# Smaller key-value blocks that share TensorE: 60-feature groups in two column halves, and four 64x64 tiles at once

## The chip, the core and the metric

The kernel runs on one core of a Trainium2 chip. A core has five engines that run side by side: TensorE (PE in the profile; its weight loads are PEld), VectorE (DVE), ScalarE (ACT), GpSimd (POOL) and SyncE (SP), which here only issues DMAs. TensorE writes its results to PSUM, eight banks of 512 f32 columns on 128 partitions. The metric is the device time of one execution in microseconds. Before the change three runs took 263.54 to 263.64 us, the median being 263.59 us.

## What is computed

One input `x` of 2048 tokens by 640 features goes through two branches, which a gate per token mixes.

```python
g = sigmoid((x * gate_w).sum(-1, keepdims=True))
# branch A: linear attention, 32 heads of 20 features
q, k, v = x @ wqkv            # split into 32 heads
pq, pk  = phi(q), phi(k)      # phi(t) = t+1 where t > 0, else exp(t); plus 1e-6
kv = einsum("hsd,hse->hde", pk, v)      # one 20x20 matrix a head
z  = pk.sum over tokens
a  = (einsum(pq, kv) / (einsum(pq, z) + 1e-6)) @ wo
# branch B: MLP
h  = gelu(layernorm(x) @ w1);  hs = shifted(h) @ w2;  x1 = x + hs
b  = x1 + gelu(layernorm(x1) @ w3) @ w4
out = g * a + (1 - g) * b
```

The kernel never forms `v`. It sums G = x^T pk over all tokens (640x640), then takes the blocks of wv^T G that belong to one head each (`kv`), and multiplies them by the rows of `wo` of that head. The result M (640x640) turns the normalised queries straight into branch A's output: a = (pq / den) @ M.

## The kernel before

All instructions are recorded one after the other by a planner (`_Items.run`): work stands in named streams, each item with the items it depends on and a lag in us, and the planner takes the item that its own cost estimates let TensorE begin first. Each engine then carries out its list strictly in the recorded order; waits on semaphores are put in where the data or a PSUM bank demands it. SP's list is one such queue: a DMA that waits holds up every DMA recorded behind it. `bank()` and `pair()` hand out one or two PSUM banks.

The stages, in the order of TensorE's list: q and k projections with phi (up to about 54 us); the sums of G (`gt_step`, line 795); W1, with the kv products between its groups (`kvt_group`, line 950); W2 with the layernorm sums; W3 for four chunks of 512 tokens (`w3_group`); between W3's groups the products M (`m_group`); then per token tile branch A's product (`a_tile`) and W4 (`w4_tile`, line 1122), with the outputs going out by DMA. `mm_group` (line 613) issues nearly all matmuls, so that most rows of the profile carry that line.

Around the change:

- **kv.** The 640 features are cut into five groups of 120 (six heads) and one of 40 (two heads). For each group, five matmuls over the 128-row slices of `wv` and G leave a 128 by 120 block in PSUM. `lt_evac` copies it with a mask that keeps the heads' 20x20 blocks (`Lt`). The work is in two halves with a bank pair each.
- **M.** `m_group` multiplies each of the six blocks of `Lt` by its rows of `wo` (`wo_aug`, filled by `load_wvo`), 512 and 128 columns; ACT copies the result to `M_sb`, rows 0 to 119 of block j. The sixth block, 40 rows, goes to `Mt`; `m_tail` then puts 8 of its rows under each of the five blocks (rows 120 to 127) by five DMAs on SP's queue.
- **Queries.** `qn_sum` and `qn_scale` divide each query tile by its denominator on DVE and store it in the same order of features: five blocks of 120 plus 8. `qt_tile` transposes a tile by a DMA on SP's queue (`pqnT<-pq_tok`).
- **SP's queue in this stretch** also carries the transposes of the second layernorm's output, `t_xn` (`xnT<-xn`), 16 tiles, which W3 reads. POOL computes each tile (`normalize`) into one of three buffers.

`a_tile` reads all 128 rows of every block of `M_sb`, so the first of them waits for the DMAs of `m_tail`.

Of the kernel before, what the change touches and what calls it, by code (L numbers as in the profile page):

```python
# [11 lines left out]
D = 640  # L12
# [417 lines left out]
def _build(nc, A_x, A_wqkv, A_wo, B_w1, B_w2, B_w3, B_w4, gate_w, out, dbg=None, stop=None):  # L430
# [240 lines left out]
    def memset(engf, ap, val):  # L671
        return engf(lambda e: e.memset(ap, val), [], [ap])
# [53 lines left out]
    def load_wvo():  # L726
        dp = [k_done[11]]
        sch.dma("pool", wv[:, :, :], A_wqkv[:, 2 * D:3 * D].rearrange("(k p) f -> p k f", p=128), "wv", deps=dp)
        for r in range(6):
            n = min(R6, D - R6 * r)  # L730
            sch.dma("pool", wo_aug[0:n, r, :], A_wo[R6 * r:R6 * r + n, :], "wo", group_total=6, deps=dp)
# [5 lines left out]
    aselect(mask_t[0:120], ones_c[0:120, 0:120].rearrange("p (b d) -> p b d", b=6), [[-20, 6], [0, 20]], ALU.is_ge, 0, 1)  # L737
    aselect(mask[0:120], mask_t[0:120], [[20, 6], [0, 20]], ALU.is_ge, 19, -1)
    memset(pool, Lt[:], 0.0)
    memset(pool, wvf[:, KD * D:], 0.0)  # L740
    memset(pool, wo_aug[:, 5, :], 0.0)
    memset(pool, hsT[:, :, 0:4], 0.0)
    memset(pool, hsT[:, :, S:S + 4], 0.0)


    tags = {}
# [187 lines left out]
    kv_bank = {}  # L934

    def kvt_group(h):
        b = pair()
        kv_bank[h] = b
        bank_hold.update((b, b + 1))
        mms = []  # L940
        for q_, r in enumerate(range(4) if h == 0 else range(4, 6)):
            n = min(R6, D - R6 * r)
            for k in range(KD):
                mms.append((ps[:, b, R6 * q_:R6 * q_ + n], wvf[:, D * k + R6 * r:D * k + R6 * r + 128], GT[:, k, R6 * r:R6 * r + n],
                            q_ == 0 and k == 0, k == KD - 1))

        def fn(e):
            ins = None
            for o, l, r_, st_, sp_ in mms:
                ins = e.matmul(o, l, r_, start=st_, stop=sp_, skip_group_check=True)  # L950
            return ins
        pe(fn, [wvf[:, :], GT[:, :, :]], [ps[:, b, 0:480], ps[:, b + 1, 0:1]], cost=len(mms) * 60.0)

    def lt_evac(h):
        b = kv_bank[h]
        for q_, r in enumerate(range(4) if h == 0 else range(4, 6)):
            n = min(R6, D - R6 * r)
            src = ps[0:n, b, R6 * q_:R6 * q_ + n].rearrange("p (h m i) -> p h m i", m=5, i=4)
            msk = mask[0:n, 0:n // DH, :].rearrange("p h (m i) -> p h m i", i=4)
            if r < 5:  # L960
                dst = Lt[0:n, r, 0:n].rearrange("p (h m i) -> p h m i", m=5, i=4)
            else:
                dst = Lt[0:n, r, 0:n].rearrange("p (m h i) -> p h m i", m=5, i=4)
            tt(dve, dst, src, msk, ALU.mult)
        bank_hold.difference_update((b, b + 1))

    def m_group(r):
        n = min(R6, D - R6 * r)
        kr = R6 if r < 5 else 128
        b = pair()  # L970
        mm_group(ps[:, b, 0:512], [(Lt[0:kr, r, :], wo_aug[0:kr, r, 0:512])])
        mm_group(ps[:, b + 1, 0:128], [(Lt[0:kr, r, :], wo_aug[0:kr, r, 512:D])])
        src = psf[0:n, 512 * b:512 * b + D]
        dst = M_sb[0:n, r, :] if r < 5 else Mt[0:n, :]
        activation(dst, src, ACTF.Copy)

    def m_tail():
# [73 lines left out]
    def qn_scale(t):  # L1051
        sd = qn_slot[t]
        ts(dve, dnr[:, 0, sd, :], dnr[:, 0, sd, :], EPS_PHI, None, ALU.add, ALU.bypass)
        dve(lambda e: e.reciprocal(dnr[:, 1, sd, :], dnr[:, 0, sd, :]), [dnr[:, 0, sd, :]], [dnr[:, 1, sd, :]], cost=350.0)
        blk = pq_tok[:, t, :].rearrange("p (j c) -> p j c", c=128)
        main = (blk[:, :, 0:R6].rearrange("p j (a d) -> p j a d", d=DH),
                pq_tok[:, t + 1, 0:5 * R6].rearrange("p (j a d) -> p j a d", a=6, d=DH),
                dnr[:, 1, sd, 0:30].rearrange("p (j a) -> p j a", a=6).unsqueeze(3).to_broadcast([128, 5, 6, DH]), 850.0)
        tail = (blk[:, :, R6:128].rearrange("p m (h i) -> p h m i", i=4),
                pq_tok[:, t + 1, 5 * R6:D].rearrange("p (h m i) -> p h m i", h=2, i=4),  # L1060
                dnr[:, 1, sd, 30:32].unsqueeze(2).unsqueeze(3).to_broadcast([128, 2, 5, 4]), 150.0)
        for o, i0, i1, cost in (main, tail):
            dve(lambda e, o=o, i0=i0, i1=i1: e.tensor_tensor(o, i0, i1, ALU.mult),
                [i0, dnr[:, 1, sd, :]], [o], cost=cost)
# [215 lines left out]
```

## Time and profile before

| | |
|---|---|
| Median of three runs | 263.59 us |
| Profiled execution, whole time | 263.69 us |
| Its span, first to last instruction | 261.6 us |
| PE busy | 256.0 us, 98% of the span |
| DVE, ACT, POOL busy | 149.0, 106.8, 95.3 us |
| First matmul of the first `a_tile` | 140.55 us |

The profile page is of one execution; what is outside its span is 2.1 us. The timeline lists the instructions of an engine in order of time, neighbours of a kind merged: start, length, engine, line, operation, tiles, count, and in brackets how long the engine was idle before them and what ended that. `SPq` are the DMA issues on SP's queue: their length is the time that SP is taken by the issue, not the transfer. The chain is the work that ended last, followed back to the start.

### The profile page before, as it was taken

The numbers are of one execution on the slowest core, as the hardware profiler recorded it, in microseconds if no ns is written. First come the engines' busy times: TensorE is split into PE (matmuls) and PEld (weight loads), VectorE is DVE, ScalarE is ACT, GpSimd is POOL, SyncE is SP. The second block draws the span as 40 slices with busy tenths as digits, with TensorE's granted clock in tenths as the row PEclk, the third lists the DMA queues.
The fourth block names the chain that finished last, engine by engine and source line by source line (L and its number), as shares of the span: only waits on it lengthen the run. The fifth ranks groups of instructions, "written<-read, shape, count | busy, mean of one in ns | idle before, by whom it ended". The sixth has DMA issues, their size and how long they took to land.

```text
span 261.6 us, 4268 instructions
## 1 busy us (share of the span) xinstructions
PE 256.0 (98%) x1668; PEld 135.7 (52%) x1699; DVE 149.0 (57%) x267; ACT 106.8 (41%) x215; POOL 95.3 (36%) x150
## 2 busy tenths in 40 slices
PE   8999999999999999999999999999999999999996
PEld 4555555555555555554444545554455544455553
DVE  2497787899903699979995407992023410143332
ACT  1386767752355756684875140005500045100000
POOL 5003996849774018687753201230011100011000
PEclk9999999999999999999999999999999999999999
DMA  6885979660566895544766600232000020000211
GB/s 198 253 91 137 165 172 172 179 122 16 87 125 103 224 387 155 76 81 74 111 124 125 103 0 0 41 84 77 0 3 0 3 100 0 3 0 0 103 50 50
DMA packets 50612, 24.82 MB, mean 95 GB/s; under 512 B 41973, under 2 KB 49182, under 8 KB 50593
## 3 DMA queue, kind: packets, MB, share of 16 engines
q1 hardware_dynamic: 49152, 20.98, 36.6%
q0 software_dynamic: 1152, 3.28, 5.7%
q8 instruction: 13, 0.21, 0.3%
q10 hardware_dynamic: 288, 0.30, 0.3%
q14 instruction: 7, 0.05, 0.1%
HBM read 12.04 MB, written 2.62 MB: 56 GB/s over the span
## 4 chain that ended last, share of the span: by engine, by line
PE 95%; DVE 1%; DMA 1%; issue 1%; ACT 0%
PE ps L613 60%; PE ps L1122 21%; PE ps L795 8%; PE ps L874 2%; DMA x_tok<-in_A_x_dram 1%; PE ps L1036 1%; PE ps L1104 1%; DVE x_tok L652 1%; PE ps L875 1%; PE ps L624 1%; PE ps L950 1%; DVE abx L652 0%; ACT junk L668 0%; DVE xT L678 0%; PE ps L1101 0%
## 5 line engine op out<-in xcount | busy, mean ns | idle before, releaser
L613 PE MATMUL ps<-xnT,w 128*128 128x512 bf16 x348 | 80.7, 379 | 0.7 <-issue 0.2
L1122 PE MATMUL ps<-w,h2T 128*128 128x512 bf16 (+1 forms) x411 | 58.1, 298 | 0.3
L669 ACT ACTIVATE h2T<-ps 128x512 bf16<-128x512 f32 x52 | 30.4, 600 | 65.7 <-PE ps L613 65.7
L613 PEld LDWEIGHTS ps<-xnT,w 128*128 128x128 bf16 x360 | 34.0, 98 | 36.9 <-issue 0.4
L652 DVE SCALAR_TENSOR_TENSOR x_tok<-ps,stg,abx 128x512 bf16<-128x512 f32 (+1 forms) x32 | 17.2, 550 | 61.6 <-PE ps L1122 61.6
L635 POOL TENSOR_SCALAR abx<-x_tok,stg 128x640 f32<-128x640 bf16 x16 | 14.8, 927 | 101.9 <-DVE x_tok L652 95.1
L1122 PEld LDWEIGHTS ps<-w,h2T 128*128 128x128 bf16 x416 | 32.4, 98 | 25.6 <-issue 1.1
L635 POOL TENSOR_SCALAR xn<-x_tok,st 128x640 bf16<-128x640 bf16 x32 | 33.8, 1062 | 15.3 <-DMA xnT<-xn 14.8
L669 ACT ACTIVATE Er<-ps 128x640 bf16<-128x640 f32 x32 | 22.3, 705 | 18.7 <-PE ps L875 8.6
L668 ACT ACTIVATE junk<-x_tok 128x640 bf16<-128x640 bf16 x32 | 23.6, 737 | 4.8 <-DVE x_tok L650 4.3
L669 ACT ACTIVATE hsT<-ps 128x512 bf16<-128x512 f32 (+1 forms) x32 | 18.9, 594 | 15.1 <-PE ps L613 14.8
L613 PE MATMUL ps<-M_sb,pqnT 128*128 128x512 bf16 (+1 forms) x157 | 23.7, 297 | 0.2
L613 PE MATMUL ps<-w,hsT 128*128 128x128 bf16 (+1 forms) x158 | 23.7, 298 | 0.1
L795 PE MATMUL ps<-pk_tok,x_tok 128*128 128x128 bf16 (+1 forms) x156 | 23.3, 297 | 0.2
L652 DVE SCALAR_TENSOR_TENSOR abx<-ps,stg,abx 128x640 f32<-128x640 f32 x16 | 14.1, 884 | 14.6 <-PE ps L613 14.6
L613 PE MATMUL ps<-wkg,xT 128*128 128x131 bf16 (+1 forms) x148 | 22.4, 298 | 0.1
L613 PEld LDWEIGHTS ps<-w,hsT 128*128 128x128 bf16 x160 | 13.3, 98 | 12.3
L613 PEld LDWEIGHTS ps<-M_sb,pqnT 128*128 128x128 bf16 x160 | 13.1, 98 | 10.4
L613 PE MATMUL ps<-wq,xT 128*128 128x128 bf16 (+1 forms) x118 | 18.1, 298 | 0.1
L650 DVE SCALAR_TENSOR_TENSOR x_tok<-ps,x_tok 128x640 bf16<-128x640 f32 x16 | 13.1, 821 | 6.9 <-PE ps L613 6.0
L613 PEld LDWEIGHTS ps<-wkg,xT 128*128 128x128 bf16 x150 | 12.2, 98 | 9.0
L795 PEld LDWEIGHTS ps<-pk_tok,x_tok 128*128 128x128 bf16 x160 | 12.4, 98 | 8.4
(70 smaller groups left out, 231.8 us busy)
## 6 DMA issues: line engine op xcount, KB each, us to landing
w<-in_B_w_dram SPq DMA_DIRECT2D x1, 2160.0 KB, 8.5
w<-in_B_w_dram SPq DMA_DIRECT2D x1, 2080.0 KB, 14.1
x_tok<-in_A_x_dram SPq DMA_DIRECT2D x3, 640.0 KB, 5.8
out_dram<-x_tok SPq DMA_DIRECT2D x3, 640.0 KB, 3.5
w<-in_B_w_dram POOLq DMA_DIRECT2D x8, 160.0 KB, 5.1
wkg<-in_A_wqkv_dram SPq DMA_DIRECT2D x5, 160.0 KB, 4.1
wv<-in_A_wqkv_dram POOLq DMA_DIRECT2D x1, 800.0 KB, 6.2
wo_aug<-in_A_wo_dram POOLq DMA_DIRECT2D x5, 150.0 KB, 5.2
```

What stands on the lines that cost most here:

```text
L613: ins = e.matmul(out_ap, l, r, start=(i == 0), stop=(i == n - 1))
L624: ins = e.transpose(o, s_, ident[:])
L635: return engf(lambda e: e.tensor_scalar(out_ap, in_ap, s1, s2, op0, op1), rd, [out_ap], cost=cost)
L650: return dve(lambda e: e.scalar_tensor_tensor(out_ap, in0, scalar, in1, op0, op1, accum_out=accum), rd, [out_ap, accum], cost=cost + 70.0)
L652: return dve(lambda e: e.scalar_tensor_tensor(out_ap, in0, scalar, in1, op0, op1), rd, [out_ap], cost=cost)
L668: return act(lambda e: e.activation(out_ap, in_ap, func, bias=bias, scale=scale, accum_out=accum), rd, wr, cost=cost)
L669: return act(lambda e: e.activation(out_ap, in_ap, func, bias=bias, scale=scale), rd, wr, cost=cost)
L795: ins = e.matmul(o, l, r, start=(t0 + q_ == 0), stop=(t0 + q_ == NT - 1))
L874: e.matmul(ps[:, b, 0:512], l, w[:, k, 0:512], start=(k == 0), stop=(k == KD - 1))
L875: return e.matmul(ps[:, b + 1, 0:n2], l, w[:, k, 512:512 + n2], start=(k == 0), stop=(k == KD - 1))
L950: ins = e.matmul(o, l, r_, start=st_, stop=sp_, skip_group_check=True)
L1122: ins = e.matmul(o, l, r, start=False, stop=(i == KFF - 1), skip_group_check=(n0 > 0))
```

## The change

kv is cut into ten groups of 60 features (three heads) and one of 40. Two groups share a step: one has its output on PSUM partitions 0 to 63, the other on 64 to 127, both in the same columns of one bank, with 64 columns of weights each. That is 55 matmuls of 60 (the last five of 40) columns in one item with one bank, where there were 30 matmuls of 120 (40) columns in two items. The copies with the mask become four DVE instructions.

Groups 0 to 7 (24 heads) fill a 128-row, four-block square; for these `m_quads` multiplies four 64x64 blocks per step, each on its own quarter of the array: two steps of 512 columns and two of 128, sixteen matmuls in three recorded operations, into six PSUM banks held together, copied by six ACT instructions. Groups 8 and 9 and the tail block (`m_group(4)` and `m_group(5)`) stay as matmuls over the whole array.

Queries and `M_sb` now have ten blocks of 60 rows plus 4, so `m_tail` has ten DMAs of 4 rows where it had five of 8. ACT now writes whole 128-row blocks of `M_sb`, rows for the tail among them, so the ten DMAs follow ACT's writes of `M_sb`. Its place in the plan hangs on `("m", 4)`, the last M product, with a lag of 1.5 us, where it hung on `("m", 5)`, the tail block's own and the first. `wo_aug` is zeroed whole (3840 columns, not 640) and filled by seven DMAs, not six; the mask is made by five small POOL instructions, not two.

```diff
+R3 = 60
+PAIRS = ((0, 2), (1, 3), (4, 6), (5, 7), (8, 9), (10,))
...
+    def kvt_group():
+        b = bank()
...
+        for r, gs in enumerate(PAIRS):
             for k in range(KD):
+                for c, g in enumerate(gs):
+                    n = min(R3, D - R3 * g)
+                    mms.append((ps[64 * c:64 * c + 64, b, R3 * r:R3 * r + n], wvf[:, D * k + R3 * g:D * k + R3 * g + 64],
+                                GT[:, k, R3 * g:R3 * g + n], r == 0 and k == 0, k == KD - 1))
...
+    def lt_evac():
...
+        tt(dve, Lt[0:n, 5, 0:n], ps[0:n, b, 5 * R3:5 * R3 + n], mask[0:n, 0:n], ALU.mult)
+        tt(dve, Lt[:, 0:4, 0:R3], ps[:, b, 0:4 * R3].rearrange("p (r d) -> p r d", d=R3),
+           mask[:, :].unsqueeze(1).to_broadcast([128, 4, R3]), ALU.mult)
+        for c in range(2):
+            rows = slice(64 * c, 64 * c + 64)
+            tt(dve, Lt[rows, 4, 64 * c:64 * c + R3], ps[rows, b, 4 * R3:5 * R3], mask[rows, :], ALU.mult)
...
+    def m_quads():
+        b0, b1, bt = pair(), pair(), pair()
+        bs = (b0, b0 + 1, b1, b1 + 1)
...
+                for c in range(2):
+                    jobs.append((ps[64 * c:64 * c + 64, bs[2 * i + h], :], Lt[rows, 2 * i + c, 0:64],
+                                 wo_aug[rows, 2 * i + c, 0:512], True))
...
+        for j in range(4):
+            activation(M_sb[:, j, 0:512], ps[:, bs[j], :], ACTF.Copy)
+        for h in range(2):
+            activation(M_sb[:, h:4:2, 512:D], ps[:, bt + h, 0:256].rearrange("p (i n) -> p i n", n=128), ACTF.Copy)
...
     def m_tail():
-        for j in range(KD):
-            sch.dma("sp", M_sb[R6:128, j, :], Mt[8 * j:8 * j + 8, :], "mt", group_total=KD)
+        for s_ in range(2 * KD):
+            p0 = 64 * (s_ % 2) + R3
+            sch.dma("sp", M_sb[p0:p0 + 4, s_ // 2, :], Mt[4 * s_:4 * s_ + 4, :], "mt", group_total=2 * KD)
...
-    for n, r in enumerate((5, 0, 1, 2, 3, 4)):
-        IT.add("KVF", ("m", r), 0.0, lambda r=r: m_group(r), deps=[(("lt", 1), 1.0), (("w3", (1 + 3 * n) // KFF, (1 + 3 * n) % KFF), 0.0)])
-    IT.add("MT", ("mt",), 0.0, m_tail, deps=[(("m", 5), 1.5), (("t1", NT - 1), 0.0)])
+    IT.add("KVF", ("m", 5), 0.0, lambda: m_group(5), deps=[(("lt",), 1.0), (("w3", 0, 1), 0.0)])
+    IT.add("KVF", ("mq",), 0.0, m_quads, deps=[(("w3", 0, 6), 0.0)])
+    IT.add("KVF", ("m", 4), 0.0, lambda: m_group(4), deps=[(("w3", 0, 11), 0.0)])
+    IT.add("MT", ("mt",), 0.0, m_tail, deps=[(("m", 4), 1.5), (("t1", NT - 1), 0.0)])
...
-        deps = [(("qt", t), 3.0), (("w4load",), 0.0), (("m", KD - 1), 1.0), (("mt",), 2.5)]
+        deps = [(("qt", t), 3.0), (("w4load",), 0.0), (("m", 4), 1.0), (("mt",), 2.5)]
```

The lists that the planner makes of the two programs differ in little else. TensorE's has the same items in the same order, the kv products in one place and the M products in three: the tail block where it was, the quads after W3's group 9 of the first chunk, block 4 after group 1 of the second chunk (groups counted from 0). SP's list changes in the place of `m_tail`:

```
before: xnT 0-7, M_sb x5,  xnT 8-11, pqnT 0-5, xnT 12-15,          pqnT 6-14, ...
after:  xnT 0-7,           xnT 8-11, pqnT 0-5, xnT 12-14, M_sb x10, xnT 15, pqnT 6-14, ...
```

More of the change, by code (lines that the diff above doesn't have):

```diff
@@ L480, in _build @@
     ident = pa.alloc("ident", [128, 128], BF16)
-    mask = pa.alloc("mask120", [128, 6, 20], BF16)
-    mask_t = pa.alloc("mask_t", [128, 6, 20], BF16)
+    mask = pa.alloc("mask60", [128, R3], BF16)
+    mask_t = pa.alloc("mask_t", [128, 3, R3], BF16)
     negh = pa.alloc("negh", [128, 4], F32)
@@ L728, in load_wvo @@
         sch.dma("pool", wv[:, :, :], A_wqkv[:, 2 * D:3 * D].rearrange("(k p) f -> p k f", p=128), "wv", deps=dp)
-        for r in range(6):
-            n = min(R6, D - R6 * r)
-            sch.dma("pool", wo_aug[0:n, r, :], A_wo[R6 * r:R6 * r + n, :], "wo", group_total=6, deps=dp)
+        for c, r, g, m in ((0, 0, 0, 2), (1, 0, 2, 2), (0, 2, 4, 2), (1, 2, 6, 2), (0, 4, 8, 1), (1, 4, 9, 1)):
+            sch.dma("pool", wo_aug[64 * c:64 * c + R3, r:r + m, :],
+                    A_wo[R3 * g:R3 * (g + m), :].rearrange("(g p) d -> p g d", p=R3), "wo", group_total=7, deps=dp)
+        sch.dma("pool", wo_aug[0:D - 10 * R3, 5, :], A_wo[10 * R3:D, :], "wo", group_total=7, deps=dp)
     memset(pool, ones_c[:], 1.0)
@@ L736, in _build @@
     memset(pool, negh[:], -0.5)
-    aselect(mask_t[0:120], ones_c[0:120, 0:120].rearrange("p (b d) -> p b d", b=6), [[-20, 6], [0, 20]], ALU.is_ge, 0, 1)
-    aselect(mask[0:120], mask_t[0:120], [[20, 6], [0, 20]], ALU.is_ge, 19, -1)
+    for c in range(2):
+        src = ones_c[:, 0:R3].rearrange("p (b d) -> p b d", d=DH)
+        mid = mask_t[:, 2, :].rearrange("p (b d) -> p b d", d=DH)
+        dst = mask_t[:, c, :].rearrange("p (b d) -> p b d", d=DH)
+        aselect(mid, src, [[-DH, 3], [0, DH]], ALU.is_ge, -64 * c, 1)
+        aselect(dst, mid, [[DH, 3], [0, DH]], ALU.is_ge, 64 * c + DH - 1, -1)
+    tt(pool, mask[:, :], mask_t[:, 0, :], mask_t[:, 1, :], ALU.add)
     memset(pool, Lt[:], 0.0)
     memset(pool, wvf[:, KD * D:], 0.0)
-    memset(pool, wo_aug[:, 5, :], 0.0)
     memset(pool, hsT[:, :, 0:4], 0.0)
     memset(pool, hsT[:, :, S:S + 4], 0.0)
+    memset(pool, wo_aug[:], 0.0)
     tags = {}
@@ L932, in _build @@
         IT.add("GT", ("g", i), 1.36, lambda i=i: gt_step(i, NT - 5, NT), deps=[(("g0", NT - 1), 0.0)])
[L934 to L939, printed above, removed]
+    kv_bank = []
+    def kvt_group():
+        b = bank()
+        kv_bank.append(b)
+        bank_hold.add(b)
         mms = []
-        for q_, r in enumerate(range(4) if h == 0 else range(4, 6)):
-            n = min(R6, D - R6 * r)
+        for r, gs in enumerate(PAIRS):
             for k in range(KD):
-                mms.append((ps[:, b, R6 * q_:R6 * q_ + n], wvf[:, D * k + R6 * r:D * k + R6 * r + 128], GT[:, k, R6 * r:R6 * r + n],
-                            q_ == 0 and k == 0, k == KD - 1))
+                for c, g in enumerate(gs):
+                    n = min(R3, D - R3 * g)
+                    mms.append((ps[64 * c:64 * c + 64, b, R3 * r:R3 * r + n], wvf[:, D * k + R3 * g:D * k + R3 * g + 64],
+                                GT[:, k, R3 * g:R3 * g + n], r == 0 and k == 0, k == KD - 1))
         def fn(e):
@@ L951, in fn @@
             return ins
[L952 to L965, printed above, removed]
+        pe(fn, [wvf[:, :], GT[:, :, :]], [ps[:, b, 0:6 * R3]], cost=1100.0)
@@ new lines, in lt_evac @@
+    def lt_evac():
+        b = kv_bank[0]
+        n = D - 10 * R3
+        tt(dve, Lt[0:n, 5, 0:n], ps[0:n, b, 5 * R3:5 * R3 + n], mask[0:n, 0:n], ALU.mult)
[4 more added lines that the diff above has]
+            tt(dve, Lt[rows, 4, 64 * c:64 * c + R3], ps[rows, b, 4 * R3:5 * R3], mask[rows, :], ALU.mult)
+        bank_hold.discard(b)
@@ L967, in m_group @@
     def m_group(r):
-        n = min(R6, D - R6 * r)
-        kr = R6 if r < 5 else 128
         b = pair()
-        mm_group(ps[:, b, 0:512], [(Lt[0:kr, r, :], wo_aug[0:kr, r, 0:512])])
-        mm_group(ps[:, b + 1, 0:128], [(Lt[0:kr, r, :], wo_aug[0:kr, r, 512:D])])
+        mm_group(ps[:, b, 0:512], [(Lt[:, r, :], wo_aug[:, r, 0:512])])
+        mm_group(ps[:, b + 1, 0:128], [(Lt[:, r, :], wo_aug[:, r, 512:D])])
+        n = 128 if r < 5 else D - 10 * R3
         src = psf[0:n, 512 * b:512 * b + D]
-        dst = M_sb[0:n, r, :] if r < 5 else Mt[0:n, :]
+        dst = M_sb[:, 4, :] if r < 5 else Mt[0:n, :]
@@ L975, in m_group, with quad, fn @@
         activation(dst, src, ACTF.Copy)
+    def m_quads():
+        b0, b1, bt = pair(), pair(), pair()
+        bs = (b0, b0 + 1, b1, b1 + 1)
+        bank_hold.update(bs + (bt, bt + 1))
+        def quad(jobs, aps):
+            def fn(e):
+                ins = None
+                for o, l, r_, st_ in jobs:
+                    ins = e.matmul(o, l, r_, start=st_, stop=True, skip_group_check=True)
+                return ins
+            pe(fn, [Lt[:, 0:4, 0:64], wo_aug[:, 0:4, :]], aps, cost=len(jobs) / 4 * nfree(jobs[0][0]) * 0.4167 + 100.0)
+        for i in range(2):
+            jobs = []
+            for h in range(2):
+                rows = slice(64 * h, 64 * h + 64)
+                for c in range(2):
+                    jobs.append((ps[64 * c:64 * c + 64, bs[2 * i + h], :], Lt[rows, 2 * i + c, 0:64],
+                                 wo_aug[rows, 2 * i + c, 0:512], True))
+            quad(jobs, [ps[:, bs[2 * i + h], :] for h in range(2)])
+        jobs = []
+        for i in range(2):
+            for h in range(2):
+                rows = slice(64 * h, 64 * h + 64)
+                for c in range(2):
+                    jobs.append((ps[64 * c:64 * c + 64, bt + h, 128 * i:128 * (i + 1)], Lt[rows, 2 * i + c, 0:64],
+                                 wo_aug[rows, 2 * i + c, 512:D], i == 0))
+        quad(jobs, [ps[:, bt + h, 0:256] for h in range(2)])
+        for j in range(4):
+            activation(M_sb[:, j, 0:512], ps[:, bs[j], :], ACTF.Copy)
+        for h in range(2):
+            activation(M_sb[:, h:4:2, 512:D], ps[:, bt + h, 0:256].rearrange("p (i n) -> p i n", n=128), ACTF.Copy)
+        bank_hold.difference_update(bs + (bt, bt + 1))
@@ L985, in zb_group @@
         copy(dve, zb[:, :], psf[:, 512 * b:512 * b + D])
-    for h in range(2):
-        IT.add("KVF", ("kvt", h), 0.0, lambda h=h: kvt_group(h), deps=[(("g", KD - 1), 1.0)])
-        IT.add("KVF", ("lt", h), 0.0, lambda h=h: lt_evac(h), deps=[(("kvt", h), 0.0)])
-    for n, r in enumerate((5, 0, 1, 2, 3, 4)):
-        IT.add("KVF", ("m", r), 0.0, lambda r=r: m_group(r), deps=[(("lt", 1), 1.0), (("w3", (1 + 3 * n) // KFF, (1 + 3 * n) % KFF), 0.0)])
-    IT.add("MT", ("mt",), 0.0, m_tail, deps=[(("m", 5), 1.5), (("t1", NT - 1), 0.0)])
+    IT.add("KVF", ("kvt",), 0.0, kvt_group, deps=[(("g", KD - 1), 1.0)])
+    IT.add("KVF", ("lt",), 0.0, lt_evac, deps=[(("kvt",), 0.0)])
+    IT.add("KVF", ("m", 5), 0.0, lambda: m_group(5), deps=[(("lt",), 1.0), (("w3", 0, 1), 0.0)])
+    IT.add("KVF", ("mq",), 0.0, m_quads, deps=[(("w3", 0, 6), 0.0)])
+    IT.add("KVF", ("m", 4), 0.0, lambda: m_group(4), deps=[(("w3", 0, 11), 0.0)])
+    IT.add("MT", ("mt",), 0.0, m_tail, deps=[(("m", 4), 1.5), (("t1", NT - 1), 0.0)])
     IT.add("ZB", ("zb",), 0.0, zb_group, deps=[(("z", NT - 1), 1.7), (("w2", 0), 0.0)])
@@ L1054, in qn_scale @@
         dve(lambda e: e.reciprocal(dnr[:, 1, sd, :], dnr[:, 0, sd, :]), [dnr[:, 0, sd, :]], [dnr[:, 1, sd, :]], cost=350.0)
[L1055 to L1060, printed above, removed]
+        blk = pq_tok[:, t, :].rearrange("p (s c) -> p s c", c=64)
+        main = (blk[:, :, 0:R3].rearrange("p s (a d) -> p s a d", d=DH),
+                pq_tok[:, t + 1, 0:10 * R3].rearrange("p (s a d) -> p s a d", a=3, d=DH),
+                dnr[:, 1, sd, 0:30].rearrange("p (s a) -> p s a", a=3).unsqueeze(3).to_broadcast([128, 10, 3, DH]), 850.0)
+        tail = (blk[:, :, R3:64].rearrange("p (h m) i -> p h m i", m=5),
+                pq_tok[:, t + 1, 10 * R3:D].rearrange("p (h m i) -> p h m i", h=2, i=4),
                 dnr[:, 1, sd, 30:32].unsqueeze(2).unsqueeze(3).to_broadcast([128, 2, 5, 4]), 150.0)
@@ L1181, in _build @@
             if c == 0 and j == 0:
-                deps0 = [(("kvt", 1), 0.0), (("z", NT - 1), 1.5)]
+                deps0 = [(("kvt",), 0.0), (("z", NT - 1), 1.5)]
             else:
```

3 lines of the change are left out of this document (1 added, 2 removed).

## The prediction

> **What bounds the kernel now.** I read the page's busy times and chain first, then the chain in the stretch of the kv products, then the timelines of PE, SP and POOL around the first `a_tile`, and last the groups by form for prices.
>
> ```profile
> span 261.6 us, 4268 instructions
> PE 256.0 (98%) x1668; PEld 135.7 (52%) x1699; DVE 149.0 (57%) x267; ACT 106.8 (41%) x215; POOL 95.3 (36%) x150
> ...
> PE 95%; DVE 1%; DMA 1%; issue 1%; ACT 0%
> ```
>
> PE is the bound from end to end: a microsecond taken off its list is worth one, and one in which it waits costs one. So the change has two sides: the matmuls it saves, and whether anything PE waits for becomes later. The second is read from SP's queue:
>
> ```profile
> 117.55 3.49 SPq L286 DMA_DIRECT2D M_sb<-Mt  x5
> 121.08 5.63 SPq L282 DMA_TRANSPOSE xnT<-xn  x4
> 126.75 7.89 SPq L282 DMA_TRANSPOSE pqnT<-pq_tok  x6
> 135.17 5.17 SPq L282 DMA_TRANSPOSE xnT<-xn  x4
> 140.40 34.09 SPq L282 DMA_TRANSPOSE pqnT<-pq_tok  x9
> ```
>
> From 117 to 142 us SP issues without a pause worth the name: a transpose holds it 1.32 us (7.89/6), a copy into `M_sb` 0.70 us (five from 117.55 to 121.08). The five copies are out at 121, some 19 us before their reader:
>
> ```profile
> 127.30 0.44 PE L613 MATMUL ps<-wo_aug,Lt 120*128 120x512 bf16 x2
> 127.57 1.24 PE L613 MATMUL ps<-xnT,w 128*128 128x512 bf16 x5
> ...
> 134.60 0.44 PE L613 MATMUL ps<-wo_aug,Lt 120*128 120x512 bf16 x2
> ...
> 140.55 1.52 PE L613 MATMUL ps<-M_sb,pqnT 128*128 128x512 bf16 x10
> ```
>
> The last row begins with the first `a_tile`, at 140.55 us: the reader of the copied rows.
>
> **The copies on SP.** They go from 5 to 10, and from ahead of xnT 8 to between xnT 14 and 15. They also wait now for ACT's writes of `M_sb`; the last of these follows the M product that ran at 134.6, and is over some 2 us later, before SP gets there, so it is the queue that sets their time. When does SP arrive? POOL's rows give the start:
>
> ```profile
> 119.77 2.61 POOL L635 TENSOR_SCALAR xn<-x_tok,st 128x640 bf16<-128x640 bf16 x3
> ...
> 130.87 3.81 POOL L635 TENSOR_SCALAR xn<-x_tok,st 128x640 bf16<-128x640 bf16 x3
> ```
>
> xn 8 is there at 119.77 + 2.61/3 = 120.6, so without the five copies ahead of it xnT 8 goes out at 120.6 instead of 121.08. Thirteen transposes (xnT 8-11, pqnT 0-5, xnT 12-14) by 1.32 make 17.2, to 137.8; xn 14, ready at 134.7, does not hold them. Before xnT 12 SP stood still for 0.5 (126.75 + 7.89 to 135.17), which I keep: 138.3, less the 0.3 that kv gives below: 138.0. The tenth copy is issued nine steps of 0.70 later, 144.3. Its landing: the view of DMA issues gives none for the copies, so I take near sizes and the transposes for ends.
>
> ```profile
> out_dram<-x_tok SPq DMA_DIRECT2D x1, 160.0 KB, 1.8
> M_sb<-Mt SPq DMA_DIRECT2D x5, 10.0 KB
> out_dram<-x_tok SPq DMA_DIRECT2D x1, 32.0 KB, 1.6
> ...
> xnT<-xn SPq DMA_TRANSPOSE x32, 2.7
> ```
>
> 1.6 to 2.7; I take 1.8, by the small plain copies. The first `a_tile` waits for all ten: 144.3 + 1.8 = 146.1 instead of 140.55, **5.6 us later**. Everything behind it in PE's list waits too, and all of that is PE's own work, so nothing pays it back. The price of a 4-row copy is not in the trace. Its nearest row is the 8-row copy; the far end is SP's cheapest plain issue, 2.33/5 = 0.47 a step, which takes 2.1 off:
>
> ```profile
> 4.55 2.33 SPq L286 DMA_DIRECT2D wkg<-in_A_wqkv_dram  x5
> ```
>
> Queued behind the copies are xnT 15 (out at 145.0, landed by 147.7; its first reader, the W3 half group, ran at 150.4 and moves later with PE) and pqnT 6-14 (first out at 146.3; its reader, `a_tile` 6, stands behind three W4 tiles): no further wait.
>
> **kv.** Thirty matmuls took 1.05 + 0.38 = 1.43 us of the chain, 0.052 each at 120 columns (rows at 77.85 and 79.97).
>
> ```profile
> 71.09 3.88 PE ps L613 x18
> ...
> 77.85 1.05 PE ps L950 x20
> ...
> 79.97 0.38 PE ps L950 x10
> ...
> 150.46 2.28 PE ps L1036 x20
> ...
> L613 PE MATMUL ps<-xnT,w 128*128 128x512 bf16 x348 | 80.7, 379 | 0.7 <-issue 0.2
> L950 PEld LDWEIGHTS ps<-GT,wv 128*128 128x128 bf16 x30 | 1.6, 98 | 0.5 <-issue 0.3
> L1036 PEld LDWEIGHTS ps<-xnT,w 128*64 128x64 bf16 x20 | 1.0, 110 | 1.2 <-issue 0.4
> ```
>
> Now 55 of 60 columns. Half the columns is 0.026 each: 1.43 if none overlap. The W3 half group shows that two 64-column halves do overlap: 20 matmuls of 512 columns in 2.28, 0.114 each, where a full-width one is spaced (1.24 - 0.38)/4 = 0.215 in the row at 127.57. Fully paired, 28 steps by 0.026 make 0.73. Upper end: each keeps 0.052, as if the step were set by loading weights and not by columns: 2.9. So -0.7 to +1.5; I take -0.3, since short steps leave little to hide 55 weight loads under. kv lies ahead of W2 and so of POOL's sums and SP's chain: it moves the whole sum. The Trainium skill, TensorEngine Tiling, Restrictions, says that column tiling switches off the fast weight load; by TensorE: Matmul & The Clock Gate, LDWEIGHTS, 64 columns then load in 64/1.2 = 53 ns, an estimate of 2.9 us for 55 in a row, the upper end.
>
> The rows for M and for what lies off the path:
>
> ```profile
> 126.21 3.02 ACT L669 ACTIVATE h2T<-ps 128x512 bf16<-128x512 f32 x6
> ...
> L669 ACT ACTIVATE M_sb<-ps 120x640 bf16<-120x640 f32 x5 | 3.6, 720 | 0.0
> L643 DVE TENSOR_TENSOR Lt<-ps,mask 120x120 bf16<-120x120 f32 x5 | 1.1, 276 | 8.0 <-PE ps L950 8.0
> L1063 DVE TENSOR_TENSOR pq_tok<-pq_tok,dnr 128x600 bf16<-128x600 bf16 x16 | 13.4, 837 | 0.6
> L1063 DVE TENSOR_TENSOR pq_tok<-pq_tok,dnr 128x40 bf16<-128x40 bf16 x16 | 3.1, 191 | 0.0
> L672 POOL MEMSET wo_aug<- 128x640 bf16 x1 | 0.6, 632 | 0.0
> L286 POOL DMA_DIRECT2D wo_aug<-in_A_wo_dram x6 | 3.3, 560 | 0.0
> ...
> 18.93 0.26 POOL L635 TENSOR_SCALAR st<-lr 128x4 f32<-128x4 f32 x1 [14.81 <-ACT lr L669]
> ...
> 52.45 1.20 SPq L282 DMA_TRANSPOSE xnT<-xn  x1
> ```
>
> **M.** Out go ten matmuls of five blocks, 0.27 a block (127.30 to 127.57): 1.35. In come block 4, 0.27, and the quads: 2 steps of 0.215 and 2 of 0.055 if four tiles overlap, 0.54; unoverlapped, 4 times that, 2.2. So -0.5 to +1.1; likely -0.5. The quads need six free banks at a time when ACT is behind (the first of these rows: six W3 copies in a row, from 126.21 to 129.23), which may hold PE for up to 1.4. All of this counts **0**: it lies ahead of the first `a_tile` and beside SP's chain, so it only changes how long PE waits there. If that cover were gone it would be worth -0.5.
>
> **Off the path.** ACT: six copies and block 4, about 3.9 against 3.6, in the shadow of PE's wait. DVE: four masks for six, some 0.5 less, after waits of 8.0 for PE; the query scaling has the same 600 and 40 elements, taken at 837 and 191 ns; a block more or less could move SP's chain by a few tenths. POOL: zeroing six times as much, 3.2 more, plus three small mask instructions, inside an idle stretch of 14.8; one more DMA issue, 0.56, ahead of the first normalised tile, whose transpose goes out at 52.45 (last row), while W1 first reads it at 71.09. All 0.
>
> **PE's pace after the wait.** PE arrives at the first `a_tile` at about 140.55 - 0.3 - 0.5 = 139.7 and waits 6.4 us. Nowhere in the trace of before does it idle so long; but at the start, after no work at all, it is slow:
>
> ```profile
> 0.83 2.72 PE L847 MATMUL ps<-const-bfloat16-1.0 128*128 128x512 bf16 x6 [0.83 <-PEq L1265]
> ...
> L847 PE MATMUL ps<-const-bfloat16-1.0 128*128 128x512 bf16 x6 | 2.7, 626 | 0.8 <-PEq L1265 0.8
> ...
> 5.03 1.27 PE L624 MATMUL ps<-ident,x_tok 128*128 128x128 bf16 x10
> 6.36 0.48 PE L874 MATMUL ps<-wq,xT 128*128 128x512 bf16 x1
> 6.67 0.22 PE L875 MATMUL ps<-wq,xT 128*128 128x128 bf16 x1
> ```
>
> Six matmuls of 512 columns are spaced (2.72 - 0.63)/5 = 0.42, twice the 0.215 of later; the pace doubles at about 6.5. Half of 5.5 us of work was lost, 2.7. So the price after the wait is between 0 (the pace is kept) and 2.7; I take 2.2, nearer the start's row, since PE has as little to do in the wait as before the start. The Trainium skill, TensorE: Matmul & The Clock Gate, part 1, has a clock that halves after an idle window of about 3.4 us and returns after a busy one; by it 3.4 us or more at half pace cost at least 1.7, 270.9 in all. The start agrees with the return; no row of before shows the drop.
>
> **Sum**, on the profiled execution (263.69, 0.1 over the median of 263.59): 263.69 + 5.6 + 2.2 = 271.5, so **271.4 us** for the median.
>
> **Rivals.**
> *The wait without the slow pace*: PE resumes at full speed, 263.59 + 5.6 = 269.2. For it: within the span no matmul after the first 7 us is slow. Against: the start.
> *Narrow weight loads bind kv*: kv costs +1.5 instead of -0.3 and moves SP's chain by 1.8: 273.2. For it: the fewer columns a matmul has, the less hides a load (98 ns for 128 columns, 110 for 64). Against: the last five kv matmuls of 40 columns needed only about 0.12 in all (0.38 - 5 x 0.052), 0.024 each.
> *The copies are in time* (other side): all ten landed by 139.7, which takes SP reaching them 6.4 us sooner than I work out; then kv and M count in full, 263.59 - 0.3 - 0.5 = 262.8. For it: copies of 4 rows may issue fast and xn 8 may come earlier. Against: even at 0.47 a step they land at 144.0, and thirteen transposes ahead of them cannot be shorter than their 17.2.
>
> **Chances.** Forecast 0.62, full pace 0.20, narrow loads 0.10, copies in time 0.06; 0.02 for a wait so short that it cancels the savings. A measurement here tells about 0.2%, 0.5 us, from no change: faster 0.06, same 0.02, slower 0.92. Range: from the wait at the cheap issue and full pace, 263.6 + 5.6 - 2.1 = 267.1, to narrow loads with 0.5 more, 273.7.
>
> **What would show it.** Right: SP's copies start near 138 and are 0.7 apart; the first `a_tile` begins near 146 with PE idle some 6 us before it, released by a DMA; matmuls of 512 columns after it spaced 0.42 for some microseconds. kv's 55 matmuls take about 1.1 us, the quads about 0.54 beside any bank wait. Wrong: `a_tile` not waiting for the copies, or SP's transposes in that stretch shorter than 1.3, or a wait on PSUM banks ahead of the quads that exceeds what the copies cost.

## The result and the profile after

The changed kernel takes 270.79 us (median of 6 runs, 270.43 to 272.59) against 263.59 (6 runs, 263.51 to 265.21). The ratio is 1.0268, with an interval of 1.024 to 1.0297: slower, 7.2 us by the medians. The prediction was 271.4 in a range of 267.1 to 273.7. The profiled execution took 270.59 us, 6.90 more than the 263.69 of before.

From the page of the changed kernel, the busy times, the granted clock of TensorE in forty slices, and the chain's shares:

```profile
span 268.6 us, 4341 instructions
PE 257.4 (96%) x1700; PEld 135.4 (50%) x1732; DVE 147.9 (55%) x265; ACT 106.7 (40%) x217; POOL 100.5 (37%) x154
...
PEclk9999999999999999999996899999999999999999
...
PE 94%; DMA 2%; SPq 1%; issue 1%; DVE 1%; ACT 0%
```

PE is busy 1.4 us longer (256.0 to 257.4), but the span grew by 7.0. One place shows in the clock: slices 22 and 23 (6.7 us each, so 141 to 154 us) stand at 6 and 8. The timeline of SP's queue in the changed kernel (start, length):

```profile
125.51 7.90 SPq L283 DMA_TRANSPOSE pqnT<-pq_tok  x6
133.51 3.87 SPq L283 DMA_TRANSPOSE xnT<-xn  x3
137.84 6.40 SPq L287 DMA_DIRECT2D M_sb<-Mt  x10
144.34 1.24 SPq L283 DMA_TRANSPOSE xnT<-xn  x1
145.63 35.88 SPq L283 DMA_TRANSPOSE pqnT<-pq_tok  x9
```

Before, the copies into `M_sb` were out by 121; now SP reaches the first at 137.84 and the tenth ends at 144.24. Their reader, in PE's timeline:

```profile
128.08 0.96 PE L991 MATMUL ps<-wo_aug,Lt 64*64 64x512 bf16 x16
129.20 5.34 PE L614 MATMUL ps<-xnT,w 128*128 128x512 bf16 x24 [0.16 <-issue]
134.38 0.43 PE L614 MATMUL ps<-wo_aug,Lt 128*128 128x512 bf16 x2
134.65 5.56 PE L614 MATMUL ps<-xnT,w 128*128 128x512 bf16 x24
145.44 2.85 PE L614 MATMUL ps<-M_sb,pqnT 128*128 128x512 bf16 x10 [5.23 <-DMA M_sb<-Mt]
148.08 2.10 PE L614 MATMUL ps<-xnT,w 128*128 128x512 bf16 x5
150.02 1.52 PE L614 MATMUL ps<-M_sb,pqnT 128*128 128x512 bf16 x10
```

PE's last matmul ahead of them ends at 145.44 - 5.23 = 140.21, and PE stands for 5.23 us. The first `a_tile` begins at 145.44, 4.89 later than the 140.55 of before, and then takes 2.85 instead of 1.52; the W3 group behind it takes 2.10 where such a group takes 1.24. The second `a_tile` has its old 1.52 again. The chain of the changed kernel (start, length, what), first at kv and then in that stretch, where its links are the copies' issues, the landing of the last, and PE:

```profile
77.74 1.05 PE ps L958 x55
78.79 0.16 issue
...
139.77 0.12 SPq L287
...
143.04 0.58 SPq L287
143.62 0.04 issue
143.66 1.73 DMA M_sb<-Mt
145.39 0.05 issue
145.44 10.27 PE ps L614 x48
...
157.50 2.28 PE ps L1077 x20
```

The last row is the W3 half group (the part of W3 that runs on half-width tiles), at 150.46 before: 7.04 later. Of these 4.89 are the wait and 7.04 - 4.89 = 2.15 the slow pace behind it. The stretches of the changed kernel with the granted clock (window, its length, busy time of PE, PEld, DVE, ACT and POOL, the clock, DMA share, GB/s):

```profile
140.00:145.40 5.40, 0.21 (x1) 0.00 (x0) 0.00 (x0) 0.60 (x1) 0.00 (x0) 0.78 0.03 8
145.40:147.00 1.60, 1.56 (x4) 0.57 (x5) 0.00 (x0) 0.00 (x0) 0.00 (x0) 0.50 0.59 112
147.00:149.90 2.90, 2.90 (x12) 1.38 (x11) 0.88 (x1) 0.00 (x0) 0.59 (x1) 0.52 0.76 137
149.90:152.00 2.10, 2.10 (x15) 1.07 (x14) 0.42 (x1) 0.60 (x1) 0.20 (x1) 1.00 0.81 82
```

A mean of 0.78 over the first 5.40 is half clock for its last 2.4, from about 143.0; the third row's 0.52 puts the return at about 149.8. PE worked at half pace from 145.44 to 149.8, and half of those 4.4 us was lost: 2.2.

The products themselves are little beside that. The first two rows of the chain have kv: 55 matmuls in 1.05, then 0.16 in which PE has no record. Against 1.43 of before, with 0.06 of such a gap there, 0.28 is saved. PE did not stand in these gaps: each hides a W1 matmul that the trace lacks (the profile page counts 1700 matmuls for 1732 weight loads). W1's weights are loaded from 78.72 on, but the first recorded W1 matmul starts at 78.95; before the change it is 80.18 and 80.42. Since one is lacking on each side, the difference holds.

### The profile page after: what moved, and what is told of

Same layout as the page of the kernel before. It is cut to its first block, busy times and chain, and to the rows that moved or that the text cites. A ratio compares the mean times of both kernels' runs of the same rounds, so it can differ in the third digit from the quotient of the medians.

```text
span 268.6 us, 4341 instructions
## 1 busy us (share of the span) xinstructions
PE 257.4 (96%) x1700; PEld 135.4 (50%) x1732; DVE 147.9 (55%) x265; ACT 106.7 (40%) x217; POOL 100.5 (37%) x154
## 4 chain that ended last, share of the span: by engine, by line
PE 94%; DMA 2%; SPq 1%; issue 1%; DVE 1%; ACT 0%
PE ps L614 59%; PE ps L1163 20%; PE ps L802 8%; PE ps L881 2%; SPq L287 1%; DMA x_tok<-in_A_x_dram 1%; DVE x_tok L653 1%; PE ps L1077 1%; PE ps L1145 1%; PE ps L625 1%; DMA M_sb<-Mt 1%; PE ps L882 1%; PE ps L958 0%; PE ps L991 0%; ACT h2T L670 0%
## 5 line engine op out<-in xcount | busy, mean ns | idle before, releaser
L614 PE MATMUL ps<-xnT,w 128*128 128x512 bf16 x352 | 81.7, 382 | 0.6 <-issue 0.2
L1163 PE MATMUL ps<-w,h2T 128*128 128x128 bf16 (+1 forms) x409 | 57.9, 298 | 0.7 <-issue 0.5
L653 DVE SCALAR_TENSOR_TENSOR x_tok<-ps,stg,abx 128x512 bf16<-128x512 f32 (+1 forms) x32 | 17.2, 550 | 61.7 <-PE ps L1163 61.6
L636 POOL TENSOR_SCALAR xn<-x_tok,st 128x640 bf16<-128x640 bf16 x32 | 36.2, 1136 | 12.7 <-DMA xnT<-xn 12.2
L614 PE MATMUL ps<-M_sb,pqnT 128*128 128x128 bf16 (+1 forms) x155 | 24.8, 307 | 5.5 <-DMA M_sb<-Mt 5.2
```

Of the source, the lines that this page charges most:

```text
L614: ins = e.matmul(out_ap, l, r, start=(i == 0), stop=(i == n - 1))
L636: return engf(lambda e: e.tensor_scalar(out_ap, in_ap, s1, s2, op0, op1), rd, [out_ap], cost=cost)
L653: return dve(lambda e: e.scalar_tensor_tensor(out_ap, in0, scalar, in1, op0, op1), rd, [out_ap], cost=cost)
L1163: ins = e.matmul(o, l, r, start=False, stop=(i == KFF - 1), skip_group_check=(n0 > 0))
```

## The experiments

**The copies early.** Only the order of the changed kernel's lists is edited: the last M product right behind the quads, eight copies behind the quads and two behind that product, all ahead of xnT 12.

```diff
-    def m_tail():
-        for s_ in range(2 * KD):
+    def m_tail(s0, s1):
+        for s_ in range(s0, s1):
...
-    IT.add("KVF", ("m", 4), 0.0, lambda: m_group(4), deps=[(("w3", 0, 11), 0.0)])
-    IT.add("MT", ("mt",), 0.0, m_tail, deps=[(("m", 4), 1.5), (("t1", NT - 1), 0.0)])
+    IT.add("KVF", ("m", 4), 0.0, lambda: m_group(4), deps=[])
+    IT.add("MT", ("mt0",), 0.0, lambda: m_tail(0, 8), deps=[(("mq",), 0.0), (("t1", NT - 1), 0.0)])
+    IT.add("MT", ("mt",), 0.0, lambda: m_tail(8, 10), deps=[(("m", 4), 0.0), (("t1", NT - 1), 0.0)])
...
-        IT.add("T2", ("t2", u), 0.0, lambda u=u: t_xn(2, u), deps=[(("n2", u), 1.1)])
+        IT.add("T2", ("t2", u), 0.0, lambda u=u: t_xn(2, u), deps=[(("n2", u), 1.1)] + ([(("mt",), None)] if u == 12 else []))
...
-        ... deps=[(("qn", t), 3.2), (("w2", NT - 1), 0.5), (("t2", 11 if t < 6 else NT - 1), 0.0)])
+        ... deps=[(("qn", t), 3.2), (("w2", NT - 1), 0.5), (("t2", 11 if t < 4 else NT - 1), 0.0)])
```

> The changed kernel with the order of recording alone altered: the last M product (block 4) directly after the quads, eight of the ten copies hung on the quads, two on block 4, and xnT 12 to 15 and pqnT 4 and 5 recorded behind the copies. SP reaches the copies after pqnT 3, near 130.5, and waits for ACT's last write of M_sb, near 132.5; ten copies by 0.62 and 1.75 of landing end near 140. Theory (the wait for the copies' place on SP and the half pace after it are the whole loss): the first a_tile begins between 139.8 and 140.5, PE waits 0.6 us at most, no half pace, time 263.1 to 263.9 us. Rival 1 (narrow tiles and quads cost PE or its clock): stays above 268 us. Rival 2 (it is the number of copies, ten issues in front of other transposes, whatever the place): the loss moves to the W3 half group that needs xnT 15, time 265 us or more.

Measured: 263.68 us against 263.64, ratio 1.0011 (0.9988 to 1.0034). The same kernel was run once more with more rounds:

> The changed kernel with the copies early, once more beside the kv part alone. It has kv's saving and the quads, and waits for PSUM banks ahead of the M products. Theory: the quads' saving is used up by these waits, so no better than the kv part alone: 263.2 us, ratio 0.9988. Rival (the quads' saving counts once the copies are early): 262.7, ratio 0.997.

263.82 against 263.58, ratio 1.0017 (1.0 to 1.0033). Timelines of SP and PE of that second run:

```profile
131.38 6.80 SPq L287 DMA_DIRECT2D M_sb<-Mt  x10
138.30 5.20 SPq L283 DMA_TRANSPOSE xnT<-xn  x4
...
128.03 0.96 PE L991 MATMUL ps<-wo_aug,Lt 64*64 64x512 bf16 x16
129.40 0.22 PE L614 MATMUL ps<-wo_aug,Lt 128*128 128x128 bf16 x1 [0.41 <-ACT h2T L670]
129.66 10.97 PE L614 MATMUL ps<-xnT,w 128*128 128x512 bf16 x49
140.47 1.52 PE L614 MATMUL ps<-M_sb,pqnT 128*128 128x512 bf16 x10
```

All new tiles, all ten copies, and no loss: the copies are issued by 138.18, the first `a_tile` begins at 140.47 without a wait and has its 1.52. So the 7 us are not in the tiles. Nor is there a gain: the time cannot be told from that of before, and the theory's 263.2 (ratio 0.9988) lies outside the interval. Block 4 right behind the quads costs two waits for ACT. The 0.41 in its row is partly work, since the record of block 4's first matmul is missing there; the trace of the first of the two runs has it:

```profile
128.87 0.45 PE L614 MATMUL ps<-wo_aug,Lt 128*128 128x512 bf16 x2 [0.18 <-ACT h2T L670]
129.36 10.96 PE L614 MATMUL ps<-xnT,w 128*128 128x512 bf16 x50
```

There block 4 starts 0.40 after the last matmul of the quads, where a W3 matmul follows them by 0.15 in the run with five copies below, and W3 goes on 0.49 after block 4's start, where 0.27 is usual (134.38 to 134.65 in the changed kernel). That is some 0.47, about what kv and M save.

**The kernel before, with its five copies late.** One dependence is edited in the kernel before, none of its tiles.

```diff
-    IT.add("MT", ("mt",), 0.0, m_tail, deps=[(("m", 5), 1.5), (("t1", NT - 1), 0.0)])
+    IT.add("MT", ("mt",), 0.0, m_tail, deps=[(("m", 4), 1.5), (("t1", NT - 1), 0.0)])
```

> The kernel before, whole array and 120-feature groups, with one edit: its five copies hang on the last M product instead of the tail block's, which records them on SP's queue behind xnT 15 and ahead of pqnT 6. Theory (the place of the copies is the loss, the tiles have no part in it): the copies start near 140.4, the fifth is issued at 143.2 and lands at 145.0; the first a_tile begins 4.4 us later than in the kernel before. PE idles 4.4 us, more than the 2.2 that kept the pace and less than the 5.2 that lost it: 268.0 us at full pace, about 270 with the half pace. Rival 1 (narrow tiles and quads are the loss): 263.6 us.

Measured: 270.48 us against 263.5, ratio 1.027 (1.0253 to 1.0287): a loss as large as the change's, with the old tiles. The profiled execution took 269.67. Its timelines of SP and PE:

```profile
134.67 5.63 SPq L282 DMA_TRANSPOSE xnT<-xn  x4
140.36 3.49 SPq L286 DMA_DIRECT2D M_sb<-Mt  x5
...
145.13 2.85 PE L613 MATMUL ps<-M_sb,pqnT 128*128 128x512 bf16 x10 [4.69 <-DMA M_sb<-Mt]
148.12 1.03 PE L613 MATMUL ps<-xnT,w 128*128 128x512 bf16 x4
```

The planner put the five behind xnT 15 here, one transpose later than the ten. The stretches of that run, columns as above:

```profile
140.40:145.10 4.70, 0.04 (x1) 0.00 (x0) 0.00 (x0) 0.60 (x1) 0.00 (x0) 0.95 0.26 43
145.10:148.00 2.90, 2.85 (x10) 1.43 (x12) 0.00 (x0) 0.00 (x0) 0.00 (x0) 0.50 0.67 128
148.00:152.00 4.00, 3.88 (x22) 1.95 (x22) 1.77 (x2) 0.98 (x2) 1.27 (x2) 1.00 0.65 124
```

Half clock from about 144.6 (0.95 over 4.70) to 148.0. The wait moved `a_tile` by 145.13 - 140.55 = 4.58, and half of the 2.87 us at half clock is 1.43: 6.0, as 269.67 - 263.69 = 5.98. That execution has a mean clock of 0.993; of the three without a trace one has 0.994 (270.35 us) and two have 0.987 (270.61 and 270.62), so that the time at half clock differs between executions of one kernel.

**Five of the ten copies.** The changed kernel, with only the copies of even number issued; it leaves out the other five.

```diff
-        for s_ in range(2 * KD):
+        for s_ in range(0, 2 * KD, 2):
...
-            sch.dma("sp", M_sb[p0:p0 + 4, s_ // 2, :], Mt[4 * s_:4 * s_ + 4, :], "mt", group_total=2 * KD)
+            sch.dma("sp", M_sb[p0:p0 + 4, s_ // 2, :], Mt[4 * s_:4 * s_ + 4, :], "mt", group_total=KD)
```

> The changed kernel with only the five copies into rows 60 to 63; those into rows 124 to 127 are left out, so part of two heads is missing from branch A. Place and waits are as in the changed kernel. Theory: the first a_tile begins 5 x 0.62 = 3.1 us earlier, near 142.3, PE waits 2.1 us. If the clock drop needs more idle time than that, time 265.5 us (270.8 - 3.1 - 2.2); if it still drops, 267.6. Rival 1 (narrow tiles): no change, 270.8.

Measured: 266.5 us against 263.64, ratio 1.0105 (1.0082 to 1.0128). The profiled execution took 265.92. Timelines of SP and PE, then the stretches:

```profile
138.39 3.30 SPq L287 DMA_DIRECT2D M_sb<-Mt  x5
...
142.90 1.53 PE L614 MATMUL ps<-M_sb,pqnT 128*128 128x512 bf16 x10 [2.17 <-DMA M_sb<-Mt]
144.27 1.24 PE L614 MATMUL ps<-xnT,w 128*128 128x512 bf16 x5
```

```profile
141.00:143.00 2.00, 0.10 (x1) 0.10 (x2) 0.00 (x0) 0.36 (x1) 0.00 (x0) 1.00 0.03 8
143.00:147.00 4.00, 4.00 (x27) 2.11 (x27) 0.98 (x2) 0.60 (x1) 0.80 (x1) 1.00 0.88 120
```

Five issues fewer shorten the wait from 5.23 to 2.17, and after 2.17 the clock is still whole in this execution: `a_tile` takes 1.53. The loss is here the wait alone, 142.90 - 140.55 = 2.35 against 265.92 - 263.69 = 2.23. The other three took 265.41 at a mean clock of 1.000 and 267.26 and 267.08 at 0.994: in two of four the clock fell for some 3 us (0.006 of 265 us, twice, since it halves). They have no trace, so that it fell in this wait is likely but not shown. The length of the wait thus hangs on the number of issues; the mean clocks suggest that the slow pace follows such a wait in some executions and not in others.

**Work for PE during the wait.** The changed kernel, with twenty matmuls on constants ahead of the first `a_tile`, so that PE waits for the same copies but hardly stands still.

```diff
+        if t == 0:
+            warmup(20 * 512, 0.0)
```

> The changed kernel with twenty matmuls of 512 columns on constants in front of the first a_tile, 4.3 us of work whose results nobody reads, in place of that much idling. Theory of the half pace as a result of idling: the first a_tile begins where it did, near 145.4, and the matmuls after it are spaced 0.215 from the first one: 270.8 - 2.2 = 268.6 us. Rival (half pace follows from the 64x64 tiles or from the wait on a DMA, not from idling): 270.8. If the dummy work delays the first a_tile by up to 0.3 us because of a bank, that much more.

Measured: 270.08 us (4 runs, 268.59 to 273.01), no clear answer: the slowest, the one profiled, was already some 4 us behind when it reached the kv products, ahead of the edit, and the other three still spread from 268.59 to 270.39 (ratio 1.0225, 1.0202 to 1.0249). So it was run again beside other kernels:

> The same kernel as e3_busy_wait once more, since the profile of that run had lost 4.5 us at 42 to 47 us to a late load and its times scatter: twenty matmuls on constants in front of the first a_tile. Theory: the first a_tile as late as in the changed kernel, matmuls behind it spaced 0.215 at once, time 268.6 us; rival (the half pace does not come from idling): 270.8.

Measured: 268.56 us (4 runs, 268.39 to 268.66) against 263.5, ratio 1.0195 (1.0179 to 1.021), clear of the 1.024 to 1.0297 of the changed kernel. Timelines of SP and PE, and one stretch:

```profile
137.71 6.39 SPq L287 DMA_DIRECT2D M_sb<-Mt  x10
...
139.73 4.54 PE L854 MATMUL ps<-const-bfloat16-1.0 128*128 128x512 bf16 x20
145.31 1.53 PE L614 MATMUL ps<-M_sb,pqnT 128*128 128x512 bf16 x10 [1.04 <-DMA M_sb<-Mt]
146.68 1.24 PE L614 MATMUL ps<-xnT,w 128*128 128x512 bf16 x5
```

```profile
145.30:149.00 3.70, 3.69 (x23) 1.92 (x24) 0.88 (x1) 0.60 (x1) 0.79 (x1) 1.00 0.95 105
```

The copies and the start of `a_tile` stay (145.31 for 145.44), the clock stays whole, and 270.79 - 268.56 = 2.23 us are back. The half pace comes from PE's standing still, not from the transfers or the wait as such.

**The kv part alone.** The kernel before with the 60-feature kv groups in two column halves; here groups 2r and 2r+1 share a step, so that `Lt` has whole blocks of two groups. M is six products as before (over 128 rows), and the queries and the five copies are those of before.

```diff
+R3 = 60
+PAIRS = ((0, 1), (2, 3), (4, 5), (6, 7), (8, 9), (10,))
...
-        for q_, r in enumerate(range(4) if h == 0 else range(4, 6)):
-            n = min(R6, D - R6 * r)
+        for r, gs in enumerate(PAIRS):
             for k in range(KD):
...
+                for c, g in enumerate(gs):
+                    n = min(R3, D - R3 * g)
+                    mms.append((ps[64 * c:64 * c + 64, b, R3 * r:R3 * r + n], wvf[:, D * k + R3 * g:D * k + R3 * g + 64],
+                                GT[:, k, R3 * g:R3 * g + n], r == 0 and k == 0, k == KD - 1))
```

> The kernel before with the kv part of the change alone: kv in 60-feature groups, two column halves at once, with the masked copies going to blocks of 120 columns, so that M, M_sb, the queries and the five early copies stay as before. wo is laid out in rows 0 to 59 and 64 to 123 by three DMAs. Theory: kv is worth what the trace of the changed kernel shows, 0.39 us, and nothing else changes: 263.2 us, ratio 0.9985. Rival 1 (narrow tiles cost more than they save): 263.6 or more. It also tells whether one half of the change beats both kernels.

Measured: 263.6 us against 263.64, ratio 0.9994 (0.9972 to 1.0015). Again with more rounds:

> The kv part alone in the kernel before, once more, on a chip whose runs of the kernel before scattered less than those beside e4_kv_only. Theory: the 0.3 us that the traces give to kv's 55 matmuls against the 30 of before, so 263.2 us where the kernel before has 263.5, ratio 0.9988; the interval should then lie within 0.2% of 1. Rival (narrow tiles give nothing): 1.000.

263.51 against 263.58, ratio 1.0011 (0.9993 to 1.003). The chain at kv in that run, and the start of its first `a_tile`:

```profile
78.16 1.05 PE ps L959 x55
79.22 0.16 issue
79.38 2.75 PE ps L615 x12
...
140.57 1.52 PE L615 MATMUL ps<-M_sb,pqnT 128*128 128x512 bf16 x9
```

The same 1.05 + 0.16 as in the changed kernel. kv starts 0.31 later in this execution (78.16 for 77.85) and the first `a_tile` only 0.02 later (140.57 for 140.55), so the saving of 0.28 stands in the trace. By time it is not shown: the expected ratio of 0.9988 lies outside the interval. In the trace of the first run kv started at 77.67, so what lies ahead of kv scatters by more than the saving.

## Why the prediction was right

**The copies on SP: right in place, 0.7 too large.** SP reached them at 137.84 (138.0 said). It began xnT 8 at 120.14, 0.2 sooner than 120.6 less the 0.3 of kv, and the thirteen transposes took 17.2 as said. The standstill of 0.5, though, was kept for the wrong place: 0.1 went by ahead of xnT 12, and 0.46 ahead of the first copy (137.38 to 137.84), though ACT's last write of `M_sb` was over at 135.77. What SP waited for there is open; that the two sizes agree is luck. The pitch was (143.66 - 137.84)/9 = 0.65, not 0.70: the mis-sized term, 9 x 0.05 = 0.5 in all; the arrival gives the rest. A 4-row copy is issued only a little faster than one of 8 rows, five of them in 3.30 against five in 3.49 in the two experiments with five; the far end of 0.47 a step was not its price. Landing and start took 145.44 - 143.66 = 1.78 (1.8 said). So +4.89 where the prediction had +5.6, and PE stood 5.23, not 6.4.

**PE's pace after the wait: right.** +2.15 measured in place (2.2 said), 2.23 by the run with work in the wait. The rival with full pace falls by these two numbers. That idling brings the slow pace was right; that its price came out at 2.2 is partly luck, as it was taken from between 0 and 2.7 by the start's row, which gave no moment of the drop. It came 2.8 us after PE stopped here (140.2 to 143.0) and 4.2 in the kernel before with late copies (140.4 to 144.6), and not within the 2.17 of the profiled run with five copies. Half clock lasted 6.8 us in the one (143.0 to 149.8) and 3.4 in the other, so the same kind of wait cost 2.2 and 1.4. The Trainium skill, TensorE: Matmul & The Clock Gate, part 1, has free-running windows of 3.413 us behind both changes; the two lengths, one window and two, agree with it. So do the mean clocks of the changed kernel's six executions, 0.987 five times and 0.993 once: over 268.6 us some 7.0 and 3.8 us at half clock. By the prediction's estimate from the Trainium skill, half pace for 3.4 us or more once PE resumes, the run of the kernel before should have lost 1.7 or more. The half clock did last 3.41, but 0.52 of it lay inside the wait, so 1.43 was lost.

The clock's own records in the traces tell more about the moment. They begin at the first stretch of full clock, 6.45 us into the span in the changed kernel and 4.66 in the kernel before with late copies (so the slow start is in no mean clock). From there to the drops it is 136.53 and 139.95 us, 40.0 and 41.0 times the 3.413 that half clock lasted in the latter; in the first run with work in the wait, where PE stood for a late load, it is 40.96, 12.0 times. So in these traces the clock changes only at ticks 3.413 us apart, and where they lie differs from execution to execution. In the changed kernel PE had stood for 2.77 us of the stretch ahead of its tick. In the kernel before with late copies a tick at 141.20, with 0.76 us of standing ahead of it, changed nothing, and the next, with a whole stretch of it, brought the drop. In the profiled run with five copies a tick at 141.98 parted the wait into 1.25 and 0.92 us, and the clock stayed. How the ticks cut a wait thus decides whether it brings the slow pace, and for how long.

**kv: right.** -0.28 (-0.3 said). Pairs do overlap: the two matmuls of a step start 4 ns apart, and steps are 31.5 ns apart, between the 26 of full pairing and the 52 that the narrow-load rival needed for each matmul. The five unpaired 40-column ones also took 31.5 each, where the same columns with 128-column weights came 25 apart in the kernel before; what sets the 31.5 is not shown. The narrow-load rival falls, and with it the estimate of 2.9 us drawn from the Trainium skill (TensorEngine Tiling, Restrictions, and TensorE: Matmul & The Clock Gate, LDWEIGHTS): all 55 took 1.05. The prediction counted 28 steps; the code makes 30, 25 pairs and five single ones.

**M: wrong in size, without weight.** From the groups of the changed kernel by form (busy us, mean ns, and the idle time before them with what ended it):

```profile
L991 PE MATMUL ps<-wo_aug,Lt 64*64 64x512 bf16 x8 | 0.6, 388 | 0.0
L991 PEld LDWEIGHTS ps<-wo_aug,Lt 64*64 64x64 bf16 x16 | 0.4, 104 | 0.8 <-ACT h2T L670 0.8
```

Four tiles do run at once (starts 3 to 4 ns apart, 0.24 us a step of 512 columns), but twice their loads wait some 0.4 for ACT's W3 copies, partly behind PE's running matmuls. So 0.89 go by from the first quad to the next weight load for the whole array (128.08 to 128.97), where 0.54 was said. The 0.16 in the row behind the quads is a missing record again: in the run with five copies that row counts 25 matmuls, not 24, and has no gap. A next matmul starts some 0.16 ahead of the end of the one before (148.08 + 2.10 = 150.18 in the timeline above, where the next starts at 150.02), so PE could have begun `a_tile` at 140.05: 0.50 sooner than before, where 139.7 was said. Of that 0.11 was there already at the start of kv (77.74 for 77.85) and 0.28 is kv's, which leaves 0.1 of the 0.5 for M. It counted 0 in the sum, since it lies ahead of a wait for something else.

**Copies in time: fell, as argued.** It needed SP at the copies 6.4 us sooner. The early-copies run gave them that by order, and even then the time was that of before, not 262.8: of the 0.8 for kv and M the trace of the changed kernel has 0.4, and in that run block 4's waits took some 0.47.

**Off the path: nothing.** POOL's zeroing took 3.3 us, the query scaling 815 and 191 ns a tile; none of it moved what lies ahead of kv.

The sum was 271.5 for the profiled execution, which took 270.59: 0.7 of the 0.9 is the wait, less than 0.1 the pace. What stays open is how much standing ahead of a tick makes the clock fall: the traces put it between 1.25 and 2.77 us, two executions with five copies, untraced, hint at 2.2 or less, and no run varied the wait's start alone.

## What to carry to other kernels

Before pricing a faster product, look where its small helpers land in a strictly ordered queue: here a change of one dependence moved some small copies behind thirteen transposes, and that outweighed every saving on TensorE. Price such copies by their number (0.6 to 0.7 us an issue here), not their bytes, and give them their place in the order by the reader's time rather than by the last writer's. A wait of TensorE that is longer than a few microseconds is to be priced with the slow pace after it, as a spread and not as one number (here nothing after 2.2 us in one trace, 1.4 and 2.2 us after some 5); if the wait cannot be removed, matmuls on constants in it gave back 2.2 us of 7.2 here.

## What the runs showed of the hardware

- TensorE's granted clock fell to 0.50 after 2.8 and 4.2 us of standing still, and came back after 6.8 and 3.4 us, of which TensorE worked 4.4 and 2.9. The price of a wait beside its length thus varied, 2.2 and 1.4 us, between much the same waits. The drops came 40.0 and 41.0 times 3.413 us after the first stretch of full clock began, so the moment is set by ticks that do not start with the wait.
- A copy of 4 rows from SBUF to SBUF holds SP 0.62 us a step, 0.80 for the first of a run; half the rows took only 0.04 off (3.30 for 3.49 over five). The last one's data are there 1.73 us after its issue starts.
- Matmuls of 40 to 60 columns with 64-column weights come at 31.5 ns a step, whether one or two share it; 40 columns with 128-column weights came at 25 ns (kernel before).
- From the last matmul on half-width or quarter tiles to the next on the whole array it is 0.12 us, start to start, behind kv (first run with early copies) and 0.15 behind the quads (run with five copies). The 0.16 of idling that the changed kernel's rows show in these places is a matmul without a record.
